# Two routing streams of an expert kernel: waits fixed when they begin, list halves and blocks set apart

## The chip, the core and the metric

The kernel runs on one core of one Trainium2 chip. The metric is the device time of one execution in microseconds (us), as the median of the runs; lower is better. TensorE is called PE in the profile, its weight loads PEld, VectorE DVE, ScalarE ACT, GpSimd POOL, and SyncE, which here only issues transfers, SP.

## The reference, cut to what matters

```python
y  = irfft(softshrink(rfft(x, axis=1) @ (w_r + i w_i) + b))       # 8 x 3072 tokens, 256 wide
h  = y @ w_in;  x2 = (h * cos(h)) @ w_out                         # 256 -> 2048 -> 256
# 8 experts, each takes exactly cap = 24576 / 8 = 3072 tokens, greedily:
logits = x2 @ w_gate
for idx in argsort(-logits.flatten()):                            # best pairs first
    tok, e = idx // 8, idx % 8
    if assigned[tok] < 0 and counts[e] < cap: assigned[tok] = e; counts[e] += 1
for e in range(8):
    out[assigned == e] = relu(x2[assigned == e] @ w1[e]) @ w2[e]  # 256 -> 1024 -> 256
```

The greedy loop is equal to eight rounds. In each one every token that is still free names its best expert that is still open; the expert that fills first at the highest threshold takes its 3072 best tokens and is closed.

## The kernel before, in words

The first 2.85 ms (function `front`) compute the transform and the dense layer; the change doesn't touch them. The rest is the function `moe`. It runs 48 blocks of 512 tokens, six for each of the eight experts. A block is eight f-steps. In each f-step PE does six matmuls `mh` (L1153, first layer, 512 columns) and twelve matmuls `mo` (L1181, second layer, 256 columns, for the f-step four earlier); two groups of four transposes `tr` (L1130) prepare the next block. What PE leaves in `mh` is taken by ScalarE (`ht`, L1163) and then VectorE (L1164), or by ScalarE twice (L1167, L1168) and GpSimd (L1169): both forms split the result of relu into a high and a low part.

Beside these blocks run two streams of routing work, written as Python generators. The main stream (`phase`) makes one round: VectorE takes each token's best open expert (`choose`, L141 to L154), PE turns the values round (L163), and 31 bisection steps find the threshold. One step is a count of half the values on VectorE (L851) and of the other half on ScalarE (L853), two small matmuls on PE that add the counts (L857, L858), and two small operations on VectorE that change the threshold (`u`, L860, and `thr`, L861). After the last step come L873, L877, L884, the ties (L925) and the update of the open experts (L946 to L949). The list stream (`rows`) makes the lists of token numbers of the chosen expert: a matmul L959, some small operations (L961 to L971), and for each of the six blocks two one-hot operations on VectorE (`OH`, L983 and L984) and two halves. Each half is a pair of PE matmuls `ls` (L991), two counts on ScalarE (`jk`, L1002) and two small operations on VectorE (`pp` and `gi`, L1005 and L1006). Both halves write the one `ls` buffer, so the second pair can't start before `pp` of the first pair has read it. The gathers of a block's tokens (L1119, GpSimd) need `gi`.

All engines work off their instructions in the order in which the program gives them out. That order is made by a small planner: it keeps a time for PE (`pe`), VectorE (`dv`) and GpSimd (`pl`) in nanoseconds, adds fixed prices with `tick`, `V` and `pool`, and after each matmul of a block resumes the stream whose due time has come. A stream that yields a time asks to be resumed when `pe` has reached it. `wait(slack)` yields until `pe` is `slack` behind `dv`. Where a block needs a list that is not made yet, `until` resumes the list stream at once, as often as it takes, and nothing of the blocks is given out between. The same is done by the loop `while lists` before each round's result is used. `ffn_relu` takes the VectorE or the GpSimd form by comparing `dv` and `pl`.

Of the kernel before, what the change touches and what calls it, by code (L numbers as in the profile page):

```python
# [764 lines left out]
def moe(tc, r, X2P, w1, w2, out, N):  # L765
# [8 lines left out]
    with ExitStack() as ctx:  # L774
# [8 lines left out]
        pe, dv, pl = [0.0], [0.0], [0.0]  # L783
# [4 lines left out]
        def V(ns, after_pe=False):  # L788
            dv[0] = max(dv[0], pe[0] + (350 if after_pe else 0)) + ns

        def wait(slack=350):

            while pe[0] < dv[0] + slack:
                yield dv[0] + slack

        def phase(ph):

            cs = rt.tile([128, 1], F32, name="cs", bufs=2)
            if ph < E - 1:
                if ph:  # L800
                    r.tiles()
                for i, (n, f) in enumerate(r.choose(slice(0, NB), False) if ph else
                                           r.choose(slice(NB - 3, NB), True)):
                    f()
                    V(n + 50 if ph else 200)
                    if ph and n > 800:
                        yield from wait(-400)
                yield from wait()
                for g in range(0, J, 4) if ph else (J - 1,):
                    p = ps.tile([128, 512], F32, name="rt", bufs=1)  # L810
# [21 lines left out]
                else:  # L832
                    nc.vector.tensor_scalar(junk, wt, 0.0, None, op0=OP.is_ge, op1=OP.add, accum_out=r.cnt[:, :1])
                    V(1730, True)
                    cols = [0]
                yield from wait()
                pc = ps.tile([128, 512], F32, name="rt", bufs=1)
                for c in cols:
# [10 lines left out]
                for k in range(30, -1, -1):  # L849
                    tb = thr.bitcast(F32)  # L850
                    nc.vector.tensor_scalar(junk[:, :H], wt[:, :H], tb, None, op0=OP.is_ge, op1=OP.add, accum_out=cnt[:, 0:1])  # L851
                    with nc.allow_low_precision(reason="whole numbers up to 768"):
                        nc.scalar.activation(junk2[:, :W - H], wt[:, H:], AF.Sign, scale=-1.0, bias=tb, accum_out=cnt2[:, 0:1])  # L853
                    V(1120)
                    yield from wait(150)
                    pc = ps.tile([128, 512], F32, name="rt", bufs=1)
                    nc.tensor.matmul(pc[:, :1], sb[:, 0], cnt[:, 0:1], start=True, stop=False)  # L857
                    nc.tensor.matmul(pc[:, :1], sb[:, 1], cnt2[:, 0:1], start=False, stop=True)  # L858

                    nc.vector.tensor_scalar(u, pc[:, :1], capS, float(1 << k), op0=OP.is_lt, op1=OP.mult)  # L860
                    nc.vector.scalar_tensor_tensor(thr, u, (1 << (k - 1)) if k else 0, thr, op0=OP.bitwise_or,  # L861
                                                   op1=OP.bitwise_xor)
                    V(560, True)
# [71 lines left out]
            else:  # L935
                nc.vector.tensor_scalar(acc, taken, 0.0, None, op0=OP.is_equal, op1=OP.add, accum_out=n3[:, 0:1])
                V(300)
            lists.append([rows(ph, acc, sc, n3), 0.0])
            resume(lists)
            if ph == 0:  # L940
# [12 lines left out]
        def rows(ph, acc, sc, n3):  # L953

            nc.vector.tensor_tensor_scan(sc, acc, acc, 0.0, op0=OP.add, op1=OP.bypass)
            V(600)
            yield from wait()
            pn = ps.tile([128, 512], F32, name="ls", bufs=1)
            nc.tensor.matmul(pn[:, 0:1], before, n3[:, 0:1], start=True, stop=True)  # L959
            off = rt.tile([128, 4], F32, name="off")  # L960
            nc.vector.tensor_copy(off[:, 0:1], pn[:, 0:1])  # L961
            nc.vector.tensor_scalar(off[:, 1:2], off[:, 0:1], -1.0 - cap // 2, None, op0=OP.add)
            nc.vector.tensor_tensor(out=off[:, 2:3], in0=off[:, 0:1], in1=n3[:, 0:1], op=OP.add)
            offb = rt.tile([128, QB], F32, name="offb")
            endb = rt.tile([128, QB], F32, name="endb")
            nc.vector.tensor_scalar(offb, t0[:, 0:QB], -512.0, off[:, 0:1], op0=OP.mult, op1=OP.add)
            nc.vector.tensor_scalar(endb, t0[:, 0:QB], -512.0, off[:, 2:3], op0=OP.mult, op1=OP.add)

            RL = rt.tile([128, NB + 2], F16, name="RL", bufs=2)
            nc.vector.tensor_scalar(RL[:, :NB], sc, off[:, 1:2], None, op0=OP.add)  # L970
            nc.vector.tensor_copy(RL[:, NB:NB + 1], pcol)  # L971
            V(1500, True)
            S = rt.tile([128, 4 * QB], F32, name="S", bufs=2)
            pp = rt.tile([128, 4 * QB], F32, name="pp", bufs=2)
            gi = rt.tile([128, 4 * QB], I32, name="gi", bufs=3)
            ni = rt.tile([128, 4 * QB], I32, name="ni", bufs=3)
            EX[ph].update(gi=gi, ni=ni)
            ji = rt.tile([128, 4 * QB], I32, name="ji")
            jf = rt.tile([128, 4 * QB], F32, name="jf")
            bi = rt.tile([128, 4 * QB], I32, name="bi")  # L980
            for b in range(QB):
                OH = rt.tile([128, 512], F16, name="OH", bufs=2)
                nc.vector.tensor_scalar(OH, t0, offb[:, b:b + 1], None, op0=OP.is_ge)  # L983
                nc.vector.scalar_tensor_tensor(OH, t0, endb[:, b:b + 1], OH, op0=OP.is_lt, op1=OP.mult)  # L984
                V(1500)
                yield from wait()
                for h in range(2):
                    q = 4 * b + 2 * h
                    p = ps.tile([128, 2, 256], F32, name="ls", bufs=1)
                    for t in range(2):  # L990
                        nc.tensor.matmul(p[:, t, :NB + 1], OH[:, (2 * h + t) * 128:(2 * h + t + 1) * 128],  # L991
                                         RL[:, :NB + 1], start=True, stop=True)
                        pe[0] += 83

                    for t in range(2):
                        jk = rt.tile([128, NB], F16, name=f"jk{t}")
                        if ph == b == t == 0:
                            nc.vector.tensor_scalar(jk, p[:, t, :NB], slotc[:, q:q + 1], None, op0=OP.is_lt, op1=OP.add,
                                                    accum_out=S[:, q:q + 1])
                            nc.vector.tensor_scalar(S[:, q:q + 1], S[:, q:q + 1], 2.0, -float(NB), op0=OP.mult, op1=OP.add)  # L1000
                        else:
                            nc.scalar.activation(jk, p[:, t, :NB], AF.Sign, scale=-1.0, bias=slotc[:, q + t:q + t + 1],  # L1002
                                                 accum_out=S[:, q + t:q + t + 1])

                    nc.vector.scalar_tensor_tensor(pp[:, q:q + 2], S[:, q:q + 2], 64.0, p[:, :, NB], op0=OP.mult, op1=OP.add)  # L1005
                    nc.vector.tensor_scalar(gi[:, q:q + 2], pp[:, q:q + 2], 64.0 * NB, None, op0=OP.add)  # L1006
                    dv[0] = max(dv[0], pe[0] + 1900) + 350
                    if ph == b == 0:
                        EARLY(h)
                    else:  # L1010
                        yield dv[0]
                READY.add((ph, b))
                if ph == b == 0:
                    yield pe[0] + 1500
                if b in (1, QB - 1):
                    s = slice(0, 8) if b == 1 else slice(8, 4 * QB)

                    nc.vector.tensor_scalar(ji[:, s], pp[:, s], 64.0 * NB - 47.5, 1.0 / 96, op0=OP.add, op1=OP.mult)
                    nc.vector.tensor_scalar(bi[:, s], ji[:, s], -15.5, 1.0 / 32, op0=OP.add, op1=OP.mult)
                    nc.vector.tensor_scalar(jf[:, s], bi[:, s], 3040.0, 2048.0 * NB, op0=OP.mult, op1=OP.add)  # L1020
                    nc.vector.scalar_tensor_tensor(jf[:, s], ji[:, s], -3071.0, jf[:, s], op0=OP.mult, op1=OP.add)
                    nc.vector.scalar_tensor_tensor(ni[:, s], pp[:, s], 32.0, jf[:, s], op0=OP.mult, op1=OP.add)
                    V(1000)
                    OUT.update((ph, x) for x in range(QB) if (x < 2) == (b == 1))
                yield pe[0] + (7000 if b or ph else 0)

        def routing():
            for ph in range(E):

                while at_g[0] <= (ph - 2) * QB:  # L1030
                    yield pe[0] + 1000
                yield from phase(ph)
# [181 lines left out]
        def EARLY(h):  # L1214
            gather(0, 0, (2 * h, 2 * h + 1))
# [10 lines left out]
        for i in range(n + 8):  # L1226
            g, f = divmod(i, 8)
            ph, b = divmod(g, QB)
# [85 lines left out]
```

## Time and profile before

| | us |
|---|---|
| median of 3 runs (4346.54 to 4350.93) | 4346.61 |
| profiled execution, device time | 4345.28 |
| profiled execution, span on the core | 4343.2 |
| PE busy | 4083.7 (94%) |
| VectorE busy | 3066.1 (71%) |
| ScalarE busy | 2597.5 (60%) |
| GpSimd busy | 1893.9 (44%) |

The busy shares are means over two parts of the program with different limits. The first 2.85 ms have PE busy nearly always; the expert part, from about 2960 us on, does not, and the routing streams run only in its first 34 of 48 blocks. So its rows are read by stretch. A line such as L991 is a line of the kernel; in the changed kernel the same lines stand one or two further down.

### The profile page before, as it was taken

The page shows a single profiled execution, that of the slowest core. Times are in us where ns is not written, and L with a number is a line of the kernel's source. Part 1 is how long each engine was busy: PE and PEld are TensorE (multiplying, and loading weights), DVE is VectorE, ACT ScalarE, POOL GpSimd, SP SyncE. Part 2 cuts the span into 40 slices and gives each one's busy share as a digit, 9 for nine tenths or more (in the row PEclk, how much of TensorE's full clock was granted, in tenths as well). Part 3 has the DMA queues.
Part 4 walks back from the last instruction along what each step waited for, and adds up shares of the span by engine and source line. Part 5 has one row for each costly group of instructions (what it writes and reads, how often), then busy time and mean ns, then how long its engine had stood idle before and what let it go on. Part 6 is the DMA issues. An engine that isn't in the chain of part 4 may idle for free.

```text
span 4343.2 us, 75660 instructions
## 1 busy us (share of the span) xinstructions
PE 4083.7 (94%) x28022; PEld 3853.3 (89%) x28022; DVE 3066.1 (71%) x6311; ACT 2597.5 (60%) x5743; POOL 1893.9 (44%) x2253
## 2 busy tenths in 40 slices
PE   7999999999999999999999999966898989987998
PEld 5899999999999999999999999954677877875898
DVE  6577777777777777777777778776767767765332
ACT  3666666666666666666666666654565655654332
POOL 4344444444444444444444433323345536443442
PEclk8999999999999999999999999987999999998999
DMA  7412112111112121112111100001111111111211
GB/s 220 119 57 65 52 58 67 51 58 58 48 56 72 39 65 59 55 49 73 51 45 38 49 25 23 20 8 44 46 42 54 58 36 59 58 36 46 67 49 35
DMA packets 136928, 239.86 MB, mean 55 GB/s; under 512 B 14830, under 2 KB 91502, under 8 KB 135534
## 3 DMA queue, kind: packets, MB, share of 16 engines
q1 hardware_dynamic: 73326, 115.45, 9.2%
q0 software_dynamic: 21888, 67.13, 4.8%
q10 hardware_dynamic: 41344, 52.44, 3.8%
q8 instruction: 220, 3.60, 0.4%
q14 instruction: 150, 1.23, 0.1%
HBM read 132.21 MB, written 102.76 MB: 54 GB/s over the span
## 4 chain that ended last, share of the span: by engine, by line
PE 85%; DVE 6%; ACT 3%; issue 2%; POOL 2%; DMA 1%; ACTq 0%; SPq 0%; DVEq 0%; POOLq 0%
PE px L505 25%; PE ph L492 24%; PE mo L1181 11%; PE mh L1153 11%; PE pa L394 4%; PE pa L467 3%; PE pa L360 2%; PE pa L432 2%; ACT jk L1002 1%; PE tr L1130 1%; DVE eq L851 1%; ACT tr L853 1%; PE pa L247 1%; PE ls L991 1%; PE pa L248 1%
## 5 line engine op out<-in xcount | busy, mean ns | idle before, releaser
L520 POOL TENSOR_TENSOR sn<-sn 128x384 f32<-128x384 f32 x1024 | 867.9, 848 | 1360.0 <-ACT sn L519 1347.2
L492 PE MATMUL ph<-xt,wi 128*128 128x384 f32 x6144 | 1235.8, 336 | 0.6 <-ACT xt L475 0.6
L505 PE MATMUL px<-wo,gh 128*128 128x264 f32 x6144 | 1204.6, 291 | 0.0
L492 PEld LDWEIGHTS ph<-xt,wi 128*128 128x128 f32 x6144 | 1027.1, 188 | 2.1 <-ACT xt L475 0.8
L505 PEld LDWEIGHTS px<-wo,gh 128*128 128x128 f32 x6144 | 985.7, 188 | 19.8 <-issue 2.8
L515 DVE SCALAR_TENSOR_TENSOR kr<-kr,ph 128x384 f32<-128x384 int32 x1024 | 566.8, 554 | 606.2 <-ACT kr L511 598.3
L505 PE MATMUL px<-wo,gl 128*128 128x264 f32 x3072 | 875.9, 285 | 2.6 <-DVE gl L532 2.2
L511 ACT ACTIVATE kr<-ph 128x384 int32<-128x384 f32 x1024 | 500.7, 489 | 536.1 <-PE ph L492 532.0
L519 ACT ACTIVATE sn<-kr 128x384 f32<-128x384 f32 x1024 | 538.8, 526 | 294.4 <-DVE kr L515 281.0
L1181 PE MATMUL mo<-w2s,ht 128*128 128x256 f32 x4608 | 643.7, 289 | 0.7 <-ACT mos L1200 0.7
L1153 PE MATMUL mh<-mxt,w1s 128*128 128x512 f32 x2304 | 635.1, 406 | 9.3 <-DVE ht L1164 8.8
L1181 PEld LDWEIGHTS mo<-w2s,ht 128*128 128x128 f32 x4608 | 607.1, 193 | 22.0 <-ACT mos L1200 1.4
L532 DVE TENSOR_TENSOR gl<-g,gh 128x384 fp32r<-128x384 f32 x1024 | 624.5, 610 | 1.6 <-ACT gh L528 1.3
L505 PEld LDWEIGHTS px<-wo,gl 128*128 128x128 f32 x3072 | 578.8, 188 | 9.3 <-DVE gl L532 7.4
L524 DVE SCALAR_TENSOR_TENSOR g<-sn,ph 128x384 f32<-128x384 f32 x1024 | 560.0, 547 | 0.0
L528 ACT ACTIVATE gh<-g 128x384 fp32r<-128x384 f32 x1024 | 529.8, 517 | 2.3 <-DVE g L524 2.2
L1153 PEld LDWEIGHTS mh<-mxt,w1s 128*128 128x128 f32 x2304 | 406.9, 193 | 68.5 <-DVE ht L1164 9.4
L853 ACT ACTIVATE tr<-wt,thr 128x768 bf16<-128x768 f32 (+1 forms) x217 | 202.3, 932 | 249.4 <-DVE thr L861 226.1
L1169 POOL TENSOR_TENSOR ht<-rl,ht 128x512 fp32r<-128x512 f32 x106 | 143.2, 1352 | 355.7 <-ACT ht L1168 349.2
L1206 POOL DMA_INDIRECT out_dram<-mos,ni x192 | 194.3, 1012 | 223.7 <-ACT mos L1200 141.3
L1164 DVE SCALAR_TENSOR_TENSOR ht<-mh,ht 128x512 fp32r<-128x512 f32 x278 | 188.8, 688 | 145.6 <-ACT ht L1163 142.7
L1119 POOL DMA_INDIRECT xg<-X2P,gi x192 | 192.8, 1004 | 150.1 <-DVE gi L1006 100.2
(251 smaller groups left out, 4759.5 us busy)
## 6 DMA issues: line engine op xcount, KB each, us to landing
b<-DB SPq DMA_DIRECT2D x64, 400.0 KB
a<-DA SPq DMA_DIRECT2D x96, 256.0 KB
DB<-bst ACTq DMA_DIRECT2D x96, 256.0 KB
X2P<-x2s SPq DMA_DIRECT2D x64, 384.0 KB
xa<-in_x_dram SPq DMA_DIRECT2D x60, 384.0 KB
DA<-xs ACTq DMA_DIRECT2D x112, 200.0 KB
b<-in_moe_w_out_dram SPq DMA_DIRECT2D x8, 512.0 KB
b<-in_moe_w_in_dram SPq DMA_DIRECT2D x8, 512.0 KB
```

The costliest lines, as they stand in the source:

```text
L492: nc.tensor.matmul(p, wi[:, hw, hf, f * 128:(f + 1) * 128], xt[:, hx, hf, :], start=n == 0, stop=n == 5)
L505: nc.tensor.matmul(PX[blk, t], g[:, t * 128:(t + 1) * 128], wo[:, hw, f, :], start=f == 0 and n == 0, stop=f == 15 and n == 2)
L511: nc.scalar.activation(t.bitcast(I32), PH[i], AF.Copy, scale=1.0 / TWO_PI)
L515: nc.vector.scalar_tensor_tensor(t, t.bitcast(I32), -TWO_PI, PH[i], op0=OP.mult, op1=OP.add)
L519: nc.scalar.activation(t, R[i], AF.Sin, scale=0.5)
L520: nc.gpsimd.tensor_tensor(out=t, in0=t, in1=t, op=OP.mult)
L524: nc.vector.scalar_tensor_tensor(t, SN[i], -0.5, PH[i], op0=OP.add, op1=OP.mult)
L528: nc.scalar.activation(GH[i], R[i], AF.Copy)
L532: nc.vector.tensor_sub(GL[i], R[i], GH[i].bitcast(F32))
L853: nc.scalar.activation(junk2[:, :W - H], wt[:, H:], AF.Sign, scale=-1.0, bias=tb, accum_out=cnt2[:, 0:1])
L1153: nc.tensor.matmul(p, WH[ph, 1][:, hw, k, f * 128:(f + 1) * 128], XT[ph, b][:, hx, k], start=n == 0, stop=n == 5)
L1181: nc.tensor.matmul(PO[g, k // 2][:, k % 2], HT[i][:, hx, k * 128:(k + 1) * 128], WH[ph, 2][:, hw, f], start=f == 0 and n == 0 and k % 2 == ...
```

## The change

Four numbers and one rule of the planner are changed. `wait` fixes the time for which it waits when it begins, where before it read `dv` anew at each resumption; its usual slack goes from 350 to 600, and that of the bisection steps from 150 to 300. A list half is followed by a pause until at least 4500 behind `pe` at its matmuls, and a block's list by a pause of 3000 in place of 7000. No operation is added or taken away but through the choice in `ffn_relu`.

```diff
         def wait(slack=350):
-            while pe[0] < dv[0] + slack:
-                yield dv[0] + slack
+        def wait(slack=600):
+            t = dv[0] + slack
+            while pe[0] < t:
+                yield t
...
                     V(1120)
-                    yield from wait(150)
+                    yield from wait(300)
...
                     dv[0] = max(dv[0], pe[0] + 1900) + 350
+                    later = max(dv[0], pe[0] + 4500)
                     if ph == b == 0:
                         EARLY(h)
                     else:
-                        yield dv[0]
+                        yield later
...
-                yield pe[0] + (7000 if b or ph else 0)
+                yield pe[0] + (3000 if b or ph else 0)
```

What this does to the order is seen at three places. The first is PE at the start of the lists of the third expert (round 2). `ls_41594` and `ls_41603` are the buffers of the two halves, `OH` their one-hot tile, `n3` the counts from which L959 starts. Before:

```order
L959 MATMUL ls_41571<-n3_41388,before_33911 128x1
L991 LDWEIGHTS OH_41591
L991 MATMUL ls_41594<-RL_41581,OH_41591 128x193
L991 LDWEIGHTS OH_41591
L991 MATMUL ls_41594<-RL_41581,OH_41591 128x193
L991 LDWEIGHTS OH_41591
L991 MATMUL ls_41603<-RL_41581,OH_41591 128x193
L991 LDWEIGHTS OH_41591
L991 MATMUL ls_41603<-RL_41581,OH_41591 128x193
L1181 MATMUL mo0_41356<-w2s_39813,ht_41487 128x256 x6
```

The same place in the changed kernel, from the matmul that starts the lists to the first half:

```order
L960 MATMUL ls_41391<-n3_41293,before_33911 128x1
L1155 MATMUL mh_41387<-mxt_41093,w1s_39806 128x512 x3
L1132 MATMUL tr_41418<-mident_64,xg_41238 128x128 x4
L1183 MATMUL mo0_41430<-w2s_39809,ht_41270 128x256 x6
L1183 MATMUL mo1_41431<-w2s_39809,ht_41270 128x256 x6
L1155 MATMUL mh_41449<-mxt_41093,w1s_39806 128x512 x6
L1183 MATMUL mo0_41430<-w2s_39809,ht_41322 128x256 x6
L1183 MATMUL mo1_41431<-w2s_39809,ht_41322 128x256 x6
L1155 MATMUL mh_41477<-mxt_41093,w1s_39806 128x512 x4
L992 LDWEIGHTS OH_41411
L992 MATMUL ls_41482<-RL_41401,OH_41411 128x193
```

Thirteen `mh`, four `tr` and 24 `mo` matmuls now stand between the start and the first half, where before nothing did. The second place follows on it, from the first half to the second:

```order
L992 MATMUL ls_41482<-RL_41401,OH_41411 128x193
L1155 MATMUL mh_41477<-mxt_41093,w1s_39806 128x512 x2
L1132 MATMUL tr_41495<-mident_64,xg_41238 128x128 x4
L1183 MATMUL mo0_41430<-w2s_39809,ht_41367 128x256 x6
L1183 MATMUL mo1_41431<-w2s_39809,ht_41367 128x256 x6
L1155 MATMUL mh_41521<-mxt_41093,w1s_39806 128x512 x6
L1183 MATMUL mo0_41430<-w2s_39809,ht_41425 128x256 x6
L1183 MATMUL mo1_41431<-w2s_39809,ht_41425 128x256
L992 LDWEIGHTS OH_41411
L992 MATMUL ls_41543<-RL_41401,OH_41411 128x193
```

Eight `mh`, four `tr` and 19 `mo` matmuls stand between the halves; in the first fence the second half follows the first at once. The third place is PE between bisection steps of the second expert's round (round 1); `cnt` and `cnt2` are the counts from VectorE and ScalarE. Before:

```order
L858 MATMUL rt_39600<-cnt2_38546,sbones_38545 128x1
L1153 MATMUL mh_39596<-mxt_39200,w1s_38155 128x512 x3
L1181 MATMUL mo0_39509<-w2s_38240,ht_39504 128x256 x6
L1181 MATMUL mo1_39510<-w2s_38240,ht_39504 128x256 x6
L1153 MATMUL mh_39627<-mxt_39496,w1s_38155 128x512 x4
L857 LDWEIGHTS sbones_38545
L857 MATMUL rt_39632<-cnt_38542,sbones_38545 128x1
```

And in the changed kernel:

```order
L859 MATMUL rt_39420<-cnt2_38606,sbones_38605 128x1
L1183 MATMUL mo0_39249<-w2s_38240,ht_39317 128x256 x2
L1183 MATMUL mo1_39250<-w2s_38240,ht_39317 128x256 x6
L1155 MATMUL mh_39435<-mxt_39229,w1s_38155 128x512 x6
L858 LDWEIGHTS sbones_38605
L858 MATMUL rt_39442<-cnt_38602,sbones_38605 128x1
L859 LDWEIGHTS sbones_38605
L859 MATMUL rt_39442<-cnt2_38606,sbones_38605 128x1
L1183 MATMUL mo0_39249<-w2s_38240,ht_39348 128x256 x6
L1183 MATMUL mo1_39250<-w2s_38240,ht_39348 128x256 x6
L1155 MATMUL mh_39466<-mxt_39229,w1s_38155 128x512 x4
L858 LDWEIGHTS sbones_38605
```

Seven `mh` and twelve `mo` stood between two steps; now it is six and eight, or four and twelve.

## Rows read from the trace of the kernel before

**Rows 1.** The page: PE's busy tenths in 40 equal slices of the span.

```profile
PE   7999999999999999999999999966898989987998
```

**Rows 2.** Windows: length, busy PE, PEld, DVE, ACT, POOL (instructions); PE's clock; DMA share, GB/s.

```profile
3160.61:3847.12 686.51, 619.90 (x4091) 535.96 (x4090) 489.93 (x1121) 406.27 (x870) 345.93 (x397) 0.97 0.16 50
...
3994.38:4018.68 24.30, 24.30 (x162) 21.45 (x161) 13.47 (x23) 16.84 (x38) 15.19 (x17) 1.00 0.14 45
4114.09:4207.80 93.71, 93.71 (x610) 85.08 (x609) 31.09 (x45) 33.37 (x56) 39.24 (x55) 1.00 0.21 68
3118.59:3151.30 32.71, 13.13 (x68) 10.81 (x67) 25.01 (x64) 6.59 (x16) 9.80 (x10) 0.69 0.25 84
3951.84:3989.36 37.52, 8.47 (x33) 4.29 (x33) 18.42 (x71) 10.95 (x48) 2.91 (x5) 0.55 0.16 56
...
3541.40:3544.80 3.40, 3.40 (x13) 2.82 (x12) 2.60 (x7) 1.80 (x4) 2.61 (x3) 0.50 0.37 98
```

**Rows 3.** PE's waits, 3151.5 to 3951.5 us: us in total, times, longest us.

```profile
PE ls L991 <- DVE pp L1005: 48.7, 28, 3.3
PE ls L991 <- DVE OH L984: 13.3, 2, 8.5
...
PE rt L163 <- ACT wt L166: 4.1, 3, 2.3
PE mh L1153 <- DVE ht L1164: 3.6, 1, 3.6
```

**Rows 4.** PE's waits, 2985 to 3118.5 us.

```profile
PE ls L991 <- DVE pp L1005: 6.8, 4, 2.1
PE mh L1153 <- DVE ht L1164: 5.2, 1, 5.2
```

**Rows 5.** PE's waits, 3118.5 to 3151.5 us.

```profile
PE rt L877 <- DVE eq L873: 2.9, 1, 2.9
...
PE rt L857 <- DVE eq L851: 1.9, 1, 1.9
```

**Rows 6.** Timeline of PE at a block's start: start us, us, engine, line [idle before].

```profile
3366.16 0.33 PE L991 MATMUL ls<-RL,OH 128*128 128x193 f16 x2 [1.65 <-DVE pp L1005]
```

**Rows 7.** Timeline of PE at the start of the lists, round 1.

```profile
3135.10 0.50 PE L991 MATMUL ls<-RL,OH 128*128 128x193 f16 x2 [5.74 <-DVE OH L984]
```

**Rows 8.** Timeline of PE at the start of the lists, round 2.

```profile
3298.12 1.55 PE L1153 MATMUL mh<-mxt,w1s 128*128 128x512 f32 x6
3299.51 1.60 PE L1181 MATMUL mo<-w2s,ht 128*128 128x256 f32 x12
3300.94 1.55 PE L1153 MATMUL mh<-mxt,w1s 128*128 128x512 f32 x6
...
3313.78 0.51 PE L991 MATMUL ls<-RL,OH 128*128 128x193 f16 x2 [8.45 <-DVE OH L984]
```

**Rows 9.** Timeline of bisection steps: alone (round 0), then beside blocks (round 1).

```profile
2903.70 0.16 PE L857 MATMUL rt<-cnt,sbones 128*128 128x1 f16 x1 [1.67 <-DVE eq L851]
...
2905.56 0.16 PE L857 MATMUL rt<-cnt,sbones 128*128 128x1 f16 x1 [1.68 <-DVE eq L851]
...
3186.58 1.01 DVE L851 TENSOR_SCALAR_CACHE_REDUCE eq<-wt,thr 128x768 bf16<-128x768 f32 x1
...
3188.19 0.69 DVE L1133 TENSOR_TENSOR mxt<-tr,mxt 128x512 fp32r<-128x512 f32 x1 [0.58 <-ACT mxt L1132]
...
3189.23 1.01 DVE L851 TENSOR_SCALAR_CACHE_REDUCE eq<-wt,thr 128x768 bf16<-128x768 f32 x1
```

**Rows 10.** Timeline of GpSimd beside VectorE, then all 186 `thr`: ns, and busy us, mean ns.

```profile
3182.60 1.28 POOL L1169 TENSOR_TENSOR ht<-rl,ht 128x512 fp32r<-128x512 f32 x1 [9.64 <-ACT ht L1168]
3182.62 1.27 DVE L861 SCALAR_TENSOR_TENSOR thr<-u,thr 128x1 uint32<-128x1 uint32 x1
...
L861 DVE SCALAR_TENSOR_TENSOR thr<-u,thr x186: 158/160/1273, 3020.0 to 3936.4; 128x1 uint32<-128x1 uint32 x186
...
L861 DVE SCALAR_TENSOR_TENSOR thr<-u,thr 128x1 uint32<-128x1 uint32 x186 | 52.5, 282 | 8.1
```

More of the change, by code (lines that the diff above doesn't have):

```diff
@@ L789, in V @@
             dv[0] = max(dv[0], pe[0] + (350 if after_pe else 0)) + ns
-        def wait(slack=350):
-            while pe[0] < dv[0] + slack:
-                yield dv[0] + slack
+        def wait(slack=600):
+            t = dv[0] + slack
+            while pe[0] < t:
+                yield t
         def phase(ph):
```

## The prediction

> **What bounds the kernel now.** I began with the page's slices. PE is at nine tenths or more from slice 2 to 26, at six in the next two, and from there on between seven and nine [rows 1]. The change lies in this second part only. Next I took windows, to price a stretch with and without routing [rows 2]. Four blocks without any routing take 93.71 us, 23.43 each, and PE has no idle time in them. The 24 blocks of experts 1 to 4, beside which the rounds run, take 686.51 us; at 23.43 they would take 562.3. Of the 124 us between the two, 66.6 are idle PE (686.51 less 619.90 busy). So PE bounds the kernel, and what ends its idle time is the question. The waits of PE answer it [rows 3]: 62.0 us (48.7 + 13.3) are list matmuls, held by `pp` of the half before or by the one-hot tile; the bisection matmuls do not appear among the larger waits at all. The first expert's blocks add 6.8 us of the same kind [rows 4].
>
> The timeline shows why. At a block's start the two pairs of a list stand next to each other on PE, and the second starts 1.65 us after the first has ended, because two counts on ScalarE and `pp` lie between [rows 6]. At the start of round 2's lists it is worse: 8.45 us [rows 8]. Both come from the order: the lists were not due yet in the planner's time, a block needed them, and `until` gave them out with nothing in between. Two forced stretches are longer still: round 1 in front of expert 1 (32.71 us with 13.13 busy) and the loop that makes all of expert 6's lists at once (37.52 us with 8.47 busy) [rows 2].
>
> **The change, part by part.**
>
> *List waits, -68.8 us.* In the changed order no pair stands beside its other half outside the two forced stretches and the first block. Between the halves shown in the second place stand eight `mh`, 19 `mo` and four transposes. Six `mh` take 1.39 us start to start and twelve `mo` 1.43 [rows 8], so that is 1.85 + 2.26 = 4.1 us and the transposes; the second half needs 1.65 us after the first [rows 6]. If ScalarE has a count and a relu ahead of it, about 1.7 us more, it still fits. For the first half of a round: 13 `mh` and 24 `mo` are 3.0 + 2.9 = 5.9 us and four transposes, against 5.74 needed where nothing else was on VectorE [rows 7]; in the changed VectorE order the list's operations follow the update of the open experts with one FFN operation between them at most. So the 62.0 and the 6.8 us go. Less of it would go only where VectorE is late; that is the term of residues below. Bounds: -69 to -50.
>
> *Other waits, -12 us.* In front of expert 1 the last bisection step (1.9) and L877 (2.9) were given out by force [rows 5]; in the changed order they stand between blocks, and the small ones with them: -5.6. The waits for the turned values (4.1) and one wait of a block for its `ht` (3.6) [rows 3] come from VectorE being given too much at once at the start of a round; I let 6.4 of them and their small neighbours go. Bounds: -15 to -5.
>
> *Clock, -13 us.* PE's granted clock is 0.97 in the 686.51 us [rows 2], so about 6% of them, 41 us, were at the lower level of 1.2 GHz. One such stretch of 3.40 us shows PE busy throughout at 0.50, with 13 PE instructions; the routing-free window has 610 in 93.71, or 22 in such a time [rows 2]. It comes right behind a list gap. At half speed a busy stretch loses half its length, at most 20.6 us of the 41; the longest of them are partly idle, so I take 13, on the condition that the gaps which precede them go. Bounds: -20 to 0.
>
> *New waits of the bisection, +20 us.* This is the price. Before, a step waited until PE was behind all that VectorE had been given, later FFN operations included; now it comes sooner. In the third place, 3.05 us of matmuls between two steps (seven `mh`, twelve `mo`) become 2.34 (six and eight) or 2.36. Alone, a step takes 1.86 us; with one FFN operation on VectorE in it, which first waits 0.58 us for ScalarE, it takes 2.65 [rows 9]; with two, 2.65 + 0.69 = 3.34. I read off both orders the 180 spacings from step to step within the six rounds, priced with the two figures for matmuls, 0.12 for the step's own matmuls, and set each against what stands on VectorE. In the changed order 75 of them are too short, by 23 us in sum; before, 22 were. Spacings of 3.2 us between them give back part of it, which leaves about 13. The other part comes from GpSimd. `thr` takes 0.16 us as a rule but 1.27 when a relu subtraction runs on GpSimd; over the 186 steps the excess is 186 x (282 - 160) ns = 22.7 us [rows 10], and before, the slack swallowed nearly all of it. The planner now gives 16 more of these subtractions to GpSimd (122 for 106) and takes them from VectorE (262 for 278). Of 22.7 x 122/106 = 26 us I take a quarter, 7 us, as coming through. Queued behind a late step's L857 is everything on PE, so each microsecond counts in full. Bounds: +2 (as before) to +63 (all 180 short by 0.35: the 0.18 by which 2.65 exceeds a spacing of 2.47, and as much again for the queue on ScalarE, an estimate).
>
> The Trainium skill bears on this last point: "SBUF — State Buffer", section "Who interferes with whom", says that a VectorE instruction with two inputs in SBUF and a GpSimd instruction that reads SBUF share one port pair, and that the one which starts second stands still until the first has ended. The trace agrees: 1.27 us beside 1.28 [rows 10], and `thr` has two such inputs. By that rule alone, with no slack to swallow a hit, this term would be 13 + 26 = +39; that is the second rival below.
>
> *Residues and breaks, +8 us.* Four pairs in a block without bisection cost 24.30 - 23.43 = 0.87 us, 0.22 each, matmuls included [rows 2]; some 28 second halves now break into the blocks on their own, which may cost half of that each, 3 us. First halves whose one-hot tile is late by a fraction, 5 us. Bounds: +3 to +20.
>
> *What stays.* In both orders the tie matmul, L959 and the first block's two pairs of round 1 follow one another with no FFN matmul between them, and so do the twelve pairs of expert 6's lists. Beyond the 5.6 us above nothing comes off these two stretches. The blocks after the routing, the first 2.96 ms and the 5.2 us at the first block [rows 4] are unchanged.
>
> Sum: -68.8 - 12 - 13 + 20 + 8 = -65.8 us. From the profiled execution's 4345.28 us that gives 4279.5; the median of the runs shown lies 1.3 us above that execution, so I forecast 4281 us.
>
> **The rivals.**
>
> *Bisection becomes the bound.* If nearly every step is late, the term is +63 and not +20: 4281 + 43 = 4324 us. For it: the spacings are now within 0.3 us of what one FFN operation needs, and ScalarE has its own share (a count, then one or two relu operations) in the same queue. Against it: VectorE is busy for 489.93 of 686.51 us [rows 2], so it can catch up.
>
> *Every hit on `thr` comes through.* The steps now follow so closely that each of the 1.1 us by which a GpSimd subtraction holds up `thr` [rows 10] is waited for by PE: 26 us in place of 7, so 4281 + 19 = 4300 us. For it: 122 subtractions for 106, and steps that already need all of their spacing. Against it: two in five of the spacings are 3 us or more and have 0.4 us and over to spare. (It is the case in which the page's rule on the shared port pair sets the time.)
>
> *Nothing late at all.* Waits of the steps as before (+2), residues +3, the whole of the clock, 15 of other waits: -68.8 - 15 - 20.6 + 2 + 3 = -99, so 4247 us. The hits on `thr` speak against it.
>
> *Slower: the blocks wait for VectorE.* List and bisection operations now stand more densely ahead of `ht`; when `ht` is late, `mh` finds no free PSUM buffer. That has a price in the trace: 3.6 and 5.2 us, once each [rows 3, 4]. It would have to come in most of the 34 blocks beside the routing: at 4.4 us in 30 of them it is +132, and 4281 + 132 = 4413 us. The point from which it decides is 15 such waits, 66 us. Against it: the planner sends a relu to GpSimd when VectorE's clock runs ahead, and in 800 us there was one such wait.
>
> *It does not do what it says.* If blocks still forced their lists, the time would be about the same, 4340 to 4352. The order speaks against it: outside the named stretches a pair is forced only now and then, and then one at a time.
>
> **How the numbers follow.** Chances: the forecast 0.63, bisection the bound 0.11, every hit through 0.12, nothing late 0.09, slower 0.03, without effect 0.02. From the bounds of the terms the forecast's own range is about 4255 to 4312. To leave out no more than 2 in 10 over all cases I take 4250 to 4316, which holds most of the full-gain case and the milder part of the bisection case. What a measurement of this kernel can tell from no change is about 0.2%, 8.7 us: faster by more than that 0.95, within it 0.02, slower 0.03.
>
> **What the profile after would show.** Right: L991's wait for `pp` and `OH` falls from 62 to under 10 us in the stretch of experts 1 to 4; these 24 blocks take 615 to 645 us; the clock there is 0.98 or more; the two forced stretches are still there, the first some 5 us shorter. New among PE's waits is L858 (the old L857) behind `eq`, 10 to 30 us in all. Wrong: that wait at 50 us or more (first rival), waits of `mh` for `ht` in many blocks (third), or list pairs that still wait for `pp` in every block.

## The result and the profile after

The changed kernel takes 4310.04 us (median of 4 runs, 4308.45 to 4314.69) where the kernel before takes 4348.59 in the same comparison (4346.54 to 4350.93): a ratio of 0.9913, 95% interval 0.9896 to 0.993. It is faster by 38.5 us; the forecast was 65.8. The profiled execution took 4314.69 us (4345.28 before), so the two traces differ by 30.6 us. The part ahead of the first expert block, which the change doesn't touch, is 4.6 us longer in this execution; the expert part, from the first `mh` on, went from 1361.6 to 1326.4 us, and those 35.2 us are what has to be explained. 13.5 of them lie in the first six blocks, 13.2 in the 24 blocks of experts 1 to 4, 8.0 in the six blocks after these.

The page's slices of PE, changed kernel (against [rows 1]):

```profile
PE   7999999999999999999999999984889999997998
```

Slices 29 to 36 read 88999999 where they read 89898998; the slice at 7 behind them is still there: it holds the lists of expert 6.

Windows of the changed kernel: the 24 blocks of experts 1 to 4 (first `mh` of block 6 to first `mh` of block 30), the forced stretch of round 1, the forced stretch of expert 6's lists (columns as in [rows 2]):

```profile
3152.00:3825.35 673.35, 627.07 (x4105) 544.51 (x4104) 503.90 (x1129) 419.66 (x904) 372.79 (x414) 0.98 0.16 51
3115.23:3142.61 27.38, 12.38 (x66) 10.54 (x65) 20.22 (x53) 6.49 (x18) 8.99 (x9) 0.74 0.31 100
3901.91:3938.00 36.09, 8.04 (x32) 4.33 (x32) 17.12 (x64) 11.89 (x50) 10.46 (x13) 0.57 0.24 80
```

Against [rows 2] the 24 blocks lose 13.2 us, the forced stretches 5.3 and 1.4. Idle PE in the 24 blocks falls by 20.3 us (66.6 to 46.3), but PE is *busy* for 7.2 us more. The waits in the stretch between the two forced ones, which is the one of [rows 3]:

```profile
PE ls L992 <- DVE OH L985: 15.0, 6, 4.6
PE mo L1183 <- ACT mos L1202: 11.3, 11, 1.9
PE rt L858 <- DVE eq L852: 10.0, 17, 1.6
PE tr L1132 <- DMA xg<-X2P,gi: 4.4, 2, 4.1
PE rt L163 <- ACT wt L166: 3.6, 2, 1.8
PE mh L1155 <- DVE mxt L1135: 3.4, 2, 3.2
PE ls L992 <- DVE pp L1006: 3.2, 2, 2.8
PE mh L1155 <- DVE ht L1166: 1.0, 1, 1.0
```

The wait for `pp` has gone from 48.7 to 3.2 us, 28 times to 2. The wait for the one-hot tile, which is that of a list's *first* half, has not: 13.3 us in 2 before, 15.0 us in 6 now, each in the first three blocks of an expert. New at this size is `mo`, which finds no buffer in PSUM (the memory that PE writes) until ScalarE has emptied one into `mos`: 11.3 us. Before, in the stretch of [rows 3]:

```profile
PE mo L1181 <- ACT mos L1200: 0.3, 1, 0.3
```

One of the first halves, on PE, VectorE and GpSimd of the changed kernel:

```profile
3619.74 1.23 PE L1183 MATMUL mo<-w2s,ht 128*128 128x256 f32 x9
3625.54 0.50 PE L992 MATMUL ls<-RL,OH 128*128 128x193 f16 x2 [4.56 <-DVE OH L985]
```

```profile
3612.20 4.45 DVE L151 TENSOR_TENSOR cd<-tr 128x192 bf16<-128x192 bf16 x1
3616.68 1.23 DVE L152 TENSOR_TENSOR cd<-cd,taken 128x192 bf16<-128x192 bf16 x1
3617.95 0.96 DVE L153 TENSOR_TENSOR eq<-eq,cd 128x1536 bf16<-128x1536 bf16 x1
3618.83 1.20 DVE L1093 TENSOR_TENSOR w1s<-w1f,w1s 128x512 fp32r<-128x512 f32 x1
3619.94 2.81 DVE L154 SCALAR_TENSOR_TENSOR w<-eq,lt 128x1536 f32<-128x1536 bf16 x1
3622.67 0.47 DVE L984 TENSOR_SCALAR OH<-iota,offb 128x512 f16<-128x512 f32 x1
3623.18 2.30 DVE L985 SCALAR_TENSOR_TENSOR OH<-iota,endb,OH 128x512 f16<-128x512 f32 x1
```

```profile
3612.71 1.31 POOL L1099 TENSOR_TENSOR w2s<-w2f,w2s 128x512 fp32r<-128x512 f32 x1
3613.97 2.56 POOL L1171 TENSOR_TENSOR ht<-rl,ht 128x512 fp32r<-128x512 f32 x2
```

The list's one-hot operations stand on VectorE behind the choose operations of the next round (L151 to L154), and some of all these take far longer than usual while GpSimd works beside them; such a lengthening is called a *hold* below. L151 takes 4.45 us and ends with the third of three subtractions back to back; L985 takes 2.30 where its shortest is 0.75. In all six late first halves L985 itself is held, at 1.63 to 2.30 us, 7.6 us in sum beyond the 0.75: half as much as the 15.0 us of waiting. In the kernel before this operation never takes more than 0.77 us, and in e11 neither.

What such a wait leads to shows in the clock. The window right behind it:

```profile
3625.54:3628.90 3.36, 3.36 (x13) 3.00 (x14) 1.81 (x4) 1.51 (x5) 0.81 (x1) 0.50 0.11 39
```

PE is busy throughout at 1.2 GHz, with 13 instructions. In the 24 blocks there are 30.7 us at this level (37.5 before), in seven stretches; each has a wait of PE of 1.4 to 4.6 us shortly ahead of it, in four of the seven that of a first half of a list, in the others for `pp`, `mxt` and `mos`. Not every such wait is followed by one: the first half at 3287.50 us waits 1.48 us and the clock stays.

### The profile page after: what moved, and what is told of

Same layout as the page of the kernel before. It is cut to its first block, busy times and chain, and to the rows that moved or that the text cites. A ratio compares the mean times of both kernels' runs of the same rounds, so it can differ in the third digit from the quotient of the medians.

```text
span 4312.9 us, 75690 instructions
## 1 busy us (share of the span) xinstructions
PE 4089.1 (95%) x28022; PEld 3864.5 (90%) x28022; DVE 3068.3 (71%) x6295; ACT 2604.0 (60%) x5759; POOL 1919.7 (45%) x2269
## 4 chain that ended last, share of the span: by engine, by line
PE 80%; DVE 9%; ACT 5%; issue 3%; POOL 2%; DMA 1%; ACTq 0%; DVEq 0%; SPq 0%; POOLq 0%
PE px L505 25%; PE ph L492 24%; PE mo L1183 8%; PE mh L1155 8%; PE pa L394 5%; PE pa L467 3%; ACT tr L854 2%; PE pa L360 2%; PE pa L432 2%; DVE eq L852 1%; ACT jk L1003 1%; DVE thr L862 1%; DVE ht L1166 1%; DVE OH L985 1%; PE tr L1132 1%
## 5 line engine op out<-in xcount | busy, mean ns | idle before, releaser
L1183 PE MATMUL mo<-w2s,ht 128*128 128x256 f32 x4608 | 655.5, 289 | 11.4 <-ACT mos L1202 11.3
L1171 POOL TENSOR_TENSOR ht<-rl,ht 128x512 fp32r<-128x512 f32 x122 | 163.9, 1344 | 317.3 <-ACT ht L1170 283.4
L1166 DVE SCALAR_TENSOR_TENSOR ht<-mh,ht 128x512 fp32r<-128x512 f32 x262 | 178.0, 687 | 153.6 <-ACT ht L1165 150.8
```

Source lines behind the costliest of these rows:

```text
L1183: nc.tensor.matmul(PO[g, k // 2][:, k % 2], HT[i][:, hx, k * 128:(k + 1) * 128], WH[ph, 2][:, hw, f], start=f == 0 and n == 0 and k % 2 == ...
```

## The experiments

To compare the runs I split the 24 blocks of each trace in the same way: *length* = 562.3 (24 at 23.43) + *idle* (PE without an instruction) + *half* (half of PE's busy time at 1.2 GHz) + *rest* (routing matmuls, and what the breaks cost). The last columns are PE's waits in these blocks. Ratios are against the kernel before in the same comparison, where it took 4348.4 us (e1 to e4), 4350.1 (e5 to e8), 4364.3 (e9 to e11) and 4366.8 (e12); microseconds of different comparisons are therefore not set against each other, ratios are.

| kernel | ratio [95%] | us | length | idle | half | rest | OH | pp | L858 | mos |
|---|---|---|---|---|---|---|---|---|---|---|
| before | 1 | 4348.6 | 686.5 | 66.6 | 12.9 | 44.7 | 13.3 | 40.0 | - | 0.3 |
| changed | 0.9913 [0.9896, 0.993] | 4310.0 | 673.4 | 46.3 | 13.7 | 51.1 | 15.0 | 3.2 | 8.2 | 10.3 |
| e1 | 0.9865 [0.9849, 0.9882] | 4288.6 | 658.0 | 35.5 | 8.3 | 51.8 | 7.1 | 3.5 | 6.6 | 6.3 |
| e2 | 1.0022 [1.001, 1.0034] | 4358.6 | 693.6 | 68.3 | 18.6 | 44.5 | 19.0 | 40.9 | - | - |
| e3 | 0.9887 [0.987, 0.9903] | 4299.3 | 668.7 | 42.0 | 10.1 | 54.3 | 10.7 | - | 10.0 | 12.5 |
| e4 | 0.9879 [0.9862, 0.9895] | 4295.4 | 662.3 | 41.3 | 6.2 | 52.5 | 1.9 | 1.6 | 7.0 | 14.7 |
| e5 | 0.988 [0.9864, 0.9897] | 4298.2 | 654.2 | 35.0 | 4.7 | 52.2 | 9.9 | 2.7 | 7.2 | 7.1 |
| e6 | 0.9896 [0.988, 0.9913] | 4305.2 | 670.4 | 46.3 | 11.0 | 50.9 | - | - | 10.6 | 12.4 |
| e7 | 0.992 [0.9903, 0.9936] | 4315.7 | 683.7 | 51.7 | 11.8 | 57.9 | 6.2 | 7.5 | 14.7 | 12.4 |
| e8 | 0.9787 [0.9771, 0.9804] | 4257.7 | 655.3 | 34.6 | 6.8 | 51.6 | 7.1 | 3.5 | 6.8 | 6.5 |
| e9 | 0.9906 [0.989, 0.9923] | 4324.8 | 677.2 | 50.9 | 13.4 | 50.6 | 14.7 | 4.4 | 12.7 | 9.2 |
| e10 | 0.9902 [0.9885, 0.9918] | 4322.1 | 673.3 | 48.9 | 10.7 | 51.4 | 8.0 | 6.6 | 17.2 | 8.9 |
| e11 | 0.9956 [0.9939, 0.9973] | 4345.1 | 674.2 | 53.7 | 9.8 | 48.4 | 0.8 | - | 35.6 | 2.2 |
| e12 | 0.9852 [0.9836, 0.9868] | 4301.9 | 676.7 | 52.4 | 6.7 | 55.2 | 1.0 | 9.5 | 19.7 | 10.9 |

(A dash: not among the larger waits.)

**e1: the new wait and the new slacks, with the old pauses.** The changed kernel with the two lines of the pauses as before:

```diff
-                    later = max(dv[0], pe[0] + 4500)
-                        yield later
+                        yield dv[0]
-                yield pe[0] + (3000 if b or ph else 0)
+                yield pe[0] + (7000 if b or ph else 0)
```

> The waits alone: the wait is fixed when it begins, with the new slacks; halves and blocks follow each other as before. In its order three places are left where a list's two pairs stand together, as in the changed kernel; 35 in the kernel before. Theory A (what counts is that a list is no longer forced): nearly the whole gain, 4308 to 4322 us, with more waiting for pp because the halves stand closer. Theory B (the pauses between halves and blocks carry the gain): 4335 to 4350 us.

4288.6 us, under both ranges: better than the changed kernel by half a per cent, so that the pauses do harm in it. The waits for the lists are mostly gone without them, 10.6 us in the 24 blocks where the kernel before has 53.3:

```profile
PE ls L992 <- DVE OH L985: 7.1, 3, 3.7
PE rt L858 <- DVE eq L852: 6.6, 8, 2.0
PE mo L1182 <- ACT mos L1201: 6.3, 7, 2.0
PE ls L992 <- DVE pp L1006: 3.5, 8, 1.0
```

**e2: the pauses alone.** The kernel before with the opposite edit (4500 and 3000).

> Halves and blocks set apart (4500 and 3000), the wait read anew as before with the old slacks. Its order has 32 places where the pairs stand together. Theory A: little is gained, 4338 to 4350 us, and PE's waits for pp stay above 50 us. Theory B: 4308 to 4322 us.

4358.6 us, not faster but 0.2% slower, and over both ranges. Most pairs are still given out by force, and the wait for `pp` in the 24 blocks is what it was (40.0 us before):

```profile
PE ls L991 <- DVE pp L1005: 40.9, 22, 2.5
PE ls L991 <- DVE OH L984: 19.0, 3, 7.8
```

In the order of its PE instructions 32 list pairs still follow another pair with no FFN matmul between them (35 in the kernel before; the 11 in the loop of expert 6's lists are counted in neither). With the old wait the list stream does not come to its first half until `until` forces it, whatever the pauses say. Counted in blocks of 48 `mh`, the first half for experts 2 to 5 stands after 11.38, 17.38, 23.38 and 29.38 blocks, as in the kernel before, and always at the same point of a block, though the last bisection step came 0.8 to 1.7 blocks earlier. With the new wait (e7) it stands after 10.75, 16.0, 21.5 and 26.62, 0.7 to 0.8 blocks behind that step.

**e3: the old slacks in the changed kernel.**

```diff
-        def wait(slack=600):
+        def wait(slack=350):
-                    yield from wait(300)
+                    yield from wait(150)
```

> The changed kernel with the old slacks of 350 and 150. Spacings of bisection steps under 2.65 us: 101 of 180, in the changed kernel 81. Theory A1 (VectorE and ScalarE are late by the planner's time, so slack is worth something): bisection waits rise from 11 to 20 us or more and first halves wait longer, 4316 to 4326 us. Theory A2 (slack is idle): 4306 to 4313 us.

4299.3 us, under both ranges: no slower than the changed kernel, rather faster (the intervals overlap by 0.0007), so that A1 is refuted; whether the slack costs something, this run hardly tells. The bisection's waits are only 10.0 us with these slacks, against 8.2.

**e4: the old block pause in the changed kernel** (`3000` back to `7000`).

> The changed kernel with the pause after a block's list back at 7000. Theory A: lists are still made ahead of need, so 4306 to 4315 us. Theory B: blocks are forced again, 4320 us or more.

4295.4 us, under both ranges. The waits for the one-hot tile fall to 1.9 us and the lower clock costs 6.2 us for 13.7; `mos` rises to 14.7, and `mh` waits 9.9 us for VectorE (`mxt` and `pp`). Of the 21 us that the two pauses cost together (e1), this one accounts for about 15.

**e5: the split of the second weights on VectorE.** L1099, 512 columns of a GpSimd subtraction, goes to VectorE:

```diff
-            nc.gpsimd.tensor_tensor(out=t[:, 1, s], in0=EX[ph]['w2f'][:, s], ...
-            pool(1230)
+            dve(lambda: nc.vector.tensor_tensor(out=t[:, 1, s], in0=EX[ph]['w2f'][:, s], ...
```

> The changed kernel with the subtraction of the second layer's weight split (32 operations) moved from GpSimd to VectorE, which gets more to do. Theory L (the first halves are late because GpSimd's subtractions hold VectorE's operations): in the 24 blocks of experts 1 to 4 the time that VectorE's operations take beyond their shortest falls from 83 us to 65 or less, PE's waits for the one-hot tile there from 15.0 to under 8 us, and the time is 4294 to 4304 us. Theory V (VectorE has too much to do at the start of a round): the waits rise, 4312 to 4325 us.

4298.2 us, 0.988: the time is that of theory L, its signs are not. VectorE's time beyond the shortest duration of each kind of instruction (by line and shape), summed over the 24 blocks, is 78 us; the changed kernel has 81, or 83 as the expectation counted it, and the kernel before 54. The holds hardly became fewer, and first halves still wait 9.9 us. The order moved; the gain is small (the intervals of the two kernels just meet), and this run does not show its cause.

**e6: first halves due later.** The wait behind the one-hot tile of each list gets 2600 ns of slack:

```diff
-                yield from wait()
+                yield from wait(2600)
```

> The changed kernel with a slack of 2600 in place of 600 before the first half of each block's list. If the planner's price for the way to a first half is 2 us too low, PE's waits for the one-hot tile in the blocks of experts 1 to 4 fall from 15.0 to under 5 us and the time is 4294 to 4304 us. If the holds come in pieces of several us or the loss lies elsewhere, 4306 to 4314 us.

The waits for the one-hot tile are gone from the 24 blocks, and the time hardly moves: 4305.2 us, an interval that overlaps with that of the changed kernel. What is late next:

```profile
PE mo L1183 <- ACT mos L1202: 12.4, 13, 1.8
PE rt L858 <- DVE eq L852: 10.6, 16, 1.6
PE mh L1155 <- DVE pp L1006: 8.2, 2, 4.4
PE mh L1155 <- DVE mxt L1135: 4.3, 1, 4.3
```

`mh` now waits twice, 8.2 us, until a late `pp` is done: half of the 15.0 that were taken away.

**e7: the new wait alone**, old slacks and old pauses; the kernel before with

```diff
-            while pe[0] < dv[0] + slack:
-                yield dv[0] + slack
+            t = dv[0] + slack
+            while pe[0] < t:
+                yield t
```

> The kernel before with the wait fixed when it begins, and nothing else: old slacks, old pauses. The run with the old slacks beside the pauses was 11 us under the changed kernel. If the slack costs as much without the pauses, 4274 to 4284 us; if it only cost because the pauses had filled VectorE, 4286 to 4298 us.

4315.7 us, over both ranges, and a ratio of 0.992 where the whole change gives 0.9913: these three lines bring as much as the change. With them the forced list pairs in the order of PE fall from 35 to 3. PE's waits in the 24 blocks:

```profile
PE rt L858 <- DVE eq L852: 14.7, 15, 2.1
PE mo L1182 <- ACT mos L1201: 12.4, 13, 2.6
PE ls L992 <- DVE pp L1006: 7.5, 9, 1.9
PE ls L992 <- DVE OH L985: 6.2, 6, 2.1
```

The list waits fall from 53.3 to 13.7 us, but two thirds of that come back as waits for the bisection and `mos`, and *rest* grows by 13. So the 24 blocks are only 2.9 us shorter; the first six blocks give 12.3 us and the six after the 24 give 14.3. The four combinations with the new wait are then: old slacks and old pauses 0.992, new slacks alone added 0.9865, new pauses alone added 0.9887, both 0.9913. Added alone, the slacks help clearly and the pauses by little (the intervals of e3 and e7 meet at 0.9903); both together give no more than the new wait by itself.

**e8: e1, and each round waits for the lists before it.** At the end of a round the kernel runs what is left of the previous lists by force. Instead the round gives way until they have been given out beside blocks:

```diff
             while lists:
-                pe[0] = max(pe[0], lists[0][1])
-                resume(lists)
+                yield max(pe[0], lists[0][1]) + 500
```

> The waits alone, as in the first run, and the loop that makes all lists of expert 6 before the last round now yields until they have been made in their own time. The forced stretch cost PE some 28 us of idle time and 5 us at the lower clock. If nothing else needs those lists early: 4254 to 4264 us. If the lists of experts 6 and 7 then come too late for their blocks: 4270 us or more.

4257.7 us, a ratio of 0.9787: the fastest of all kernels here, and its interval is clear of those of both kernels. The six blocks from block 30 on take 148.28 us, 183.97 in e1. The windows, e1 first:

```profile
3802.34:3986.31 183.97, 155.56 (x1006) 135.47 (x1005) 103.64 (x280) 91.23 (x233) 70.62 (x91) 0.91 0.14 47
```

```profile
3804.22:3952.50 148.28, 147.70 (x982) 130.80 (x981) 90.62 (x220) 81.75 (x187) 76.67 (x97) 1.00 0.20 63
```

In these six blocks of e8 PE is idle for 0.6 us in sum and keeps 2.4 GHz; the forced stretch of 36 us is gone. They give 35.7 us and the 24 before them 2.6; the first six and the last twelve give 5.5 back, so that some 33 us are left.

**e9 and e10: the block pause at 1500 and at 5000** in the changed kernel.

> The changed kernel with the block pause at 1500 (changed kernel 3000, kernel before 7000). Measured so far with the new waits: 4310 at 3000, 4295 at 7000. Theory P (the pause costs by bringing first halves into the start of a round, where VectorE is held up): the cost grows as the pause shrinks, so 4310 to 4325, with 18 us or more of first-half waits (OH) of PE in blocks 6 to 29. Rival (the 15 us between 3000 and 7000 are the luck of one order, and a different order of the same kind falls elsewhere): anywhere from 4285 to 4325, with no order by the pause; a time under 4303 would be its sign.

> The changed kernel with the block pause at 5000. Theory P: between the two ends, 4298 to 4308, with 4 to 12 us of first-half waits (OH) in blocks 6 to 29. Rival (luck of the order): outside 4295 to 4310, or OH waits out of order with the pause.

By ratio the pauses of 1500, 3000, 5000 and 7000 give 0.9906, 0.9913, 0.9902 and 0.9879. (The ranges are for a kernel before at about 4349 us; on that scale 1500 gives 4308 and 5000 gives 4306.) The waits for the one-hot tile fall from 3000 on (14.7, 15.0, 8.0, 1.9 us), but at 1500 they are not the 18 us that theory P asked for. The time does not follow: the first three are the same within their intervals, and at 5000 the bisection waits 17.2 us, which takes the place of what the lists wait less. Even 7000 is set apart only from 3000, and barely (e4's interval ends at 0.9895, that of the changed kernel begins at 0.9896). So P holds in part for the wait; for the time these runs do not decide between P and the luck of one order.

**e11: no relu subtraction on GpSimd.** The planner's comparison gets a bias, so that all 384 go to VectorE:

```diff
-BIAS = 0
+BIAS = -1000000
```

> The changed kernel, but all relu subtractions go to VectorE and none to GpSimd (the planner's comparison gets a bias that VectorE always wins); the weight splits stay where they are. Theory H (GpSimd's subtractions hold VectorE up, and that is what makes first halves, bisection steps and the turned values late): VectorE's time beyond the shortest of each kind in blocks 6 to 29 falls from 83 us to under 45, and the time to 4280 to 4300, although VectorE gets 122 more operations of 0.69 us. Rival W (VectorE is simply too full at these places, held or not): those 122 operations, 84 us, make it later, mh waits for ht, 4320 to 4370.

Both theories hit one half. The hits on `thr` are gone. All `thr` of the changed kernel first, then of e11 (ns, min/median/max):

```profile
L862 DVE SCALAR_TENSOR_TENSOR thr<-u,thr x217: 158/159/1441, 2895.9 to 3892.5; 128x1 uint32<-128x1 uint32 x109
```

```profile
L862 DVE SCALAR_TENSOR_TENSOR thr<-u,thr x217: 158/159/163, 2892.6 to 3955.4; 128x1 uint32<-128x1 uint32 x109
```

VectorE's time beyond the shortest falls from 81 to 27 us, as H said. And the time is 0.9956, slower than the changed kernel, as W said (4329 on the scale of the ranges). PE's waits in the 24 blocks of e11:

```profile
PE rt L858 <- DVE eq L852: 35.6, 21, 3.5
PE mh L1155 <- DVE ht L1166: 9.8, 8, 2.0
PE mh L1155 <- DVE pp L1006: 2.3, 2, 1.3
PE mo L1183 <- ACT mos L1202: 2.2, 4, 1.0
...
PE ls L992 <- DVE OH L985: 0.8, 1, 0.8
```

First halves and `mos` are no longer late; the bisection and `ht` are. A subtraction on GpSimd can cost VectorE a hold, and without it VectorE has 0.69 us more to do, in this order where bisection steps wait for it. The run changes both at once; it shows that the holds are cheaper than the work, and does not price either. (`mos` has a second reason: a subtraction on GpSimd also costs ScalarE a copy, and ScalarE's busy time falls from 419.7 to 349.8 us. Which of the two counts, this run does not tell.)

**e12: e8 and the edit of e5.**

> The kernel of e8_waits_last_round (new wait, old pauses, and each round waits until the lists before it have been given out beside blocks) with the weight splits of e5_w2_vector as well: the subtraction of the second weights on VectorE and not on GpSimd. Theory S (the gains of the two edits add up, since the one acts on the last round and the other on the starts of rounds): in e5 the edit took 12 us off the changed kernel, so ratio 0.974 to 0.978, about 4245 us where the kernel before takes 4350. Rival O (the 12 us belong to first halves that the shorter pause had brought to the round's start, and the old pauses have taken most of these away already): no gain, ratio 0.978 to 0.982, with the bisection's waits (L858) above the 7 us of e8.

0.9852 against e8's 0.9787: the gains do not add up, neither theory's range holds it, and L858 rises from 6.8 to 19.7 us in the 24 blocks, which is the sign of rival O, and `pp` from 3.5 to 9.5. Some of it may lie in the comparison (the kernel before was slower in it too, though by 0.4% only); that has not been separated.

## Why the prediction was right, and where its size was off

The sign and the mechanism held: the second halves of the list pairs waited for `pp`, and but for 3.2 us of the 48.7 they no longer do. The time of 4310 lies in the range of 4250 to 4316, near its slow end, and by the number alone it is nearer to the rivals at 4300 and 4324 than to 4281; the rows speak against both of these. By its own steps, profiled execution against profiled execution:

| step | forecast | measured | how |
|---|---|---|---|
| list waits | -68.8, and +5 for late first halves | -50.6 | 68.8 [rows 3, 4] to 18.2 |
| other waits | -12 | -12 | round 1's stretch 5.3, expert 6's 1.4, L163 1.8, `xg` 1.8, the `mh` waits 2 |
| clock | -13 | -2.7 | half, all 36 blocks: 30.7 to 28.0; in the 24 blocks 12.9 to 13.7 |
| waits of the bisection | +20 | +11 | L858 outside the forced stretches: 10.0 and 1.2 |
| breaks | +3 | +7.4 | rest, all 36 blocks: 61.1 to 68.5 |
| waits for `mos` | none | +11 | 0.3 to 11.3 |
| sum | -65.8 | -36 | expert part measured: -35.2 |

Nearly all that is missing lies in the 24 blocks of experts 1 to 4. They were to take 615 to 645 us and take 673: 35.1 us of list waits went, but 18.2 came back at `mos` and the bisection, and 6.4 in *rest*. That the sum still fell into its range is in part luck: the bisection, forecast 9 us too dear, pays for most of the `mos` that was forgotten; with `mos` alone on top the time would have been about 4319.

*The list waits* were mis-sized in one half of them. I had one hold of 5.74 us [rows 7] as the need of a first half, "where nothing else was on VectorE", and took the planner's order for the proof that VectorE would be in time. For the first block of an expert that nearly held: two waits, 2.9 us. But the first halves of the second and third block, for which I had worked out nothing, now come at the start of the next round too, among its choose operations and weight splits, and there VectorE is neither free nor fast: four waits, 12.1 us. In all that is 15.0 us where I had allowed 5. The order shows which instruction stands behind which; it does not show that L151 takes 4.45 us there.

*The clock* failed as a step. I made it hang on the list gaps going. It is right that a lower clock follows gaps, but a few gaps of any kind are enough for it: seven stretches at 1.2 GHz before, seven after. Four of them stand behind a late first half, three behind waits for `pp` (2.79 us), `mxt` (3.17) and `mos` (1.88). Taking the late first halves away does not settle it either: with 1.9 us of them e4 still loses 6.2 us, and e6, with none, 11.0.

*`mos`* was missed. It was no wait of any size before (0.3 us). It comes with all kernels that have the new wait and GpSimd's subtractions (6.3 to 14.7 us).

*The bisection* was over-sized: 11 us. Against the rival in which every hit on `thr` comes through, the trace of the changed kernel has 22 hits with 21 us beyond the usual 0.16; 8 of them are followed by a wait of PE, 2.7 us in all, where I had let 7 come through. So the hit is mostly swallowed, and most of the waiting stands in steps without one. In e11, without a single hit, the bisection waits four times as long: there, as far as the run shows, it is the work that VectorE has to do that makes a step late. The Trainium skill, "SBUF — State Buffer", section "Who interferes with whom", says that a VectorE instruction with two inputs in SBUF and a GpSimd instruction that reads SBUF exclude one another; that `thr` falls from at most 1.44 to at most 0.163 us when the subtractions go agrees with it. That the hits set the time does not follow from it, and e11 speaks against it.

*The other rivals.* The wait of the blocks for VectorE (the slower case) came to 2.7 us for `ht` and 3.4 for `mxt` in all. Nothing late at all was too good by 63 us. That the change doesn't do what it says is refuted for the change as a whole but right for one part of it: outside the loop of expert 6 the new wait alone leaves the same 3 forced pairs, and the pauses alone leave 32 (e7, e2).

*What the profile was to show.* The forced stretches are still there and the first is 5.3 us shorter (forecast 5); the clock in the 24 blocks is 0.98; L858 waits 11 us (10 to 30). But the list waits are 18.2 and not under 10, and the 24 blocks take 673 us and not 615 to 645.

Settled: the three lines of the wait bring as much as the whole change (e7), the pauses bring nothing without them (e2) and cost beside the new slacks (e1), and one of the two forced stretches that I had left as they were held as much again (e8: 0.9787 where e1 has 0.9865). Open: why the slacks and the pauses help one by one and not together. The forced pairs are the same 3 in these orders; what differs is where VectorE's work falls, and small edits move the time by 0.2 to 0.7% (e3 to e6, e12) while one wait takes the place of another. That this is the cause is argued, not shown.

## What to carry to other kernels

A wait in a planner that looks at a running total, and not at the total when it began, chases work that is given out later; fix that first and measure it alone, before constants are tuned around it. When waits of an engine that was never the busiest go, look for what stood behind them in the queue of the next one: an order proves that the work is placed, not that the engine is on time. And one stretch in which everything is given out by force can be worth as much as many small waits: some 33 us here, by one line.

## What was not expected of the hardware

A VectorE operation can be held by several GpSimd instructions in a row: L151, at most 0.259 us in e11, took 4.45 us. It began 0.5 us ahead of three subtractions of 1.3 us back to back, beside the issue of an indirect DMA, and ended with the third of them, so that it did not get in between them. And it goes both ways: GpSimd instructions beside VectorE's operations lengthen as well (spans on GpSimd are rough). From the changed kernel, during L1093 (1.20 us from 3618.83), L154 (2.81 from 3619.94) and L985 (2.30 from 3623.18):

```profile
3618.96 2.17 POOL L1171 TENSOR_TENSOR ht<-rl,ht 128x512 fp32r<-128x512 f32 x1 [1.16 <-ACT ht L1170]
...
3621.32 2.31 POOL L1208 DMA_INDIRECT out_dram<-mos,ni  x1 [0.16 <-issue]
3623.65 1.27 POOL L1171 TENSOR_TENSOR ht<-rl,ht 128x512 fp32r<-128x512 f32 x1
```

The subtraction, 1.29 us as a rule, takes 2.17, and the issue of an indirect DMA, 0.99 as a rule, 2.31. This is no single case. Of the 408 indirect-DMA issues of the changed kernel from 2900 us on, the 248 that overlap no VectorE operation with two inputs in SBUF take 1.01 us at most; of the 160 that overlap one, 23 take more than 1.25, up to 2.52.
